# A new task order for a planned one-core kernel (long convolution, then a gated FFN)

## The chip, the core and the metric

The kernel runs on one core of a Trainium2 chip. The metric is the device time of one execution in microseconds (us): the median of three runs, 259.31 us before the change (259.17 to 259.5). The engines carry the profile's names: PE is TensorE (PEld its weight loads), DVE is VectorE, ACT is ScalarE, POOL is GpSimd, SP is SyncE, which here only issues DMAs.

## What is computed

Sequence length S = 2048, width D = 640, FFN width F = 1728, all inputs in bf16. Block A is a gated long convolution, block B a gated FFN behind a LayerNorm.

```python
def _A_ref(q, k, v, shift_k, ssm_k, ssm_D):
    k_pad = jnp.pad(k, ((0, 0), (ks - 1, 0), (0, 0)))          # ks = 4 taps
    for t in range(ks):
        k_shift = k_shift + k_pad[:, t:t + S, :] * shift_k[:, ks - 1 - t][None, None, :]
    kv = k_shift * v
    ...
    y = irfft(rfft(kv_pad) * rfft(ssm_k_pad))[:S]              # causal convolution of length S
    y = y + kv * ssm_D[None, None, :]
    return q * y

def _B_ref(x, w_gate, w_up, w_down):
    return (silu(x @ w_gate) * (x @ w_up)) @ w_down

h = x + _A_ref(_layernorm(x), A_k, A_v, A_shift_k, A_ssm_k, A_ssm_D)      # x is A_q
h2 = h + _B_ref(_layernorm(h), B_w_gate, B_w_up, B_w_down)
```

## The kernel before

The sequence is cut into four blocks of N = 512 tokens. The long convolution is done with block transforms: cosine and sine matrices (`tab` forward, `itab` inverse, `ntab` for the negated half) are multiplied on TensorE with 512 tokens at a time, and the products of transformed blocks j and filters i - j are added up on VectorE. The FFN of block i follows its part of the convolution.

All work is written as some 811 named tasks. `g.add(name, engines, fn, ...)` records one task with what it reads and writes; from that the program derives its dependencies. Nothing in the code decides when a task runs: the strings of `PLAN` do. For each engine (`pe`, `act`, `dve`, `pool`, `sp`) the plan lists task numbers in the order in which the engine runs them, and a task that names two engines ("act dve") runs on the one whose list has it. Every engine works its list strictly in order, and in front of a task it waits for the semaphores of the tasks that it depends on. A DMA belongs to the list of the engine that issues it, most of them to SP.

PSUM is cut into four units of two banks. `PLAN["units"]` gives each TensorE result tile its unit; a tile that opens a unit waits until the other engines have emptied the tile that had the unit before. `PLAN["fills"]` names tasks in front of which TensorE runs constant matmuls (128 x 512, of a tile of ones that the task `zmem` fills, line 492; the matmuls are line 497); their results are never read.

The names that matter here, with the line of the profile:

- `wb0`, `wb4` (L505): five small matmuls that spread the four tap weights of each channel; `diag0`, `diag4` (L511) turn them into diagonal matrices on VectorE. The digits 0, 2, 4 in this and the next names are chunks of 128 channels: 0 stands for chunks 0 to 3 in `wb0` and `diag0`, elsewhere 0 and 2 stand for two chunks each and 4 for one.
- `k0tC.J` (L523): the first block of k, transposed by TensorE (20 transposes); `k0e0`, `k0e2`, `k0e4` (L450, kT<-ps) copy it from PSUM to SBUF. Its data come with the DMAs `k00` and `k02`.
- `tpI.C` (L701): the short convolution of block I, matmuls with the diagonals, 28 for two chunks and 14 for one; `kv0.C` (L719) multiplies block 0 with v on VectorE. For the later blocks `keI.C` (L450, XT<-ps) and `kvI.C` (L712) do it.
- `ktM.P` (L542): the filter block M (loaded as `kcM`), transposed by TensorE, ten transposes each; `kteM.P` (L450, KT<-ps) copies it. `drowadd` (L550) adds ssm_D. `kfM` (L576) transforms the filter, `kfMe` empties PSUM (KO, C, K3r), `kbM` combines (L556).
- `xfI` (L594 for block 0, L614 later): transform of block I, `xfIe` its evacuations (XH, OS), `xbI` (L629) their combination. `pJI` (L747): products. `ybI` (L556, L646): combination ahead of the inverse.
- `ivI.J` (L894 for blocks 0 and 1, L889 later): the inverse, one tile for 128 tokens. `ivI.Je` (L904) on ScalarE evacuates; then come the residual and the LayerNorm (L911, L810, L812, L805, POOL's L807, L951), and `htI.J` transposes the result into `hnT` by a DMA that SP issues.
- `laI` (L797 to L831): first LayerNorm of a block. `xI`, `vI`, `kTI`: loads of q, v and (transposed by the DMA) k for block I.
- `fgI.HG`, `fuI.HG` (L999): gate and up matmuls of block I, half H (256 tokens), group G; 20 matmuls each, 15 for group 3, which is `fg` alone. `sg`, `su`, `sv` (L1007 to L1018) evacuate on ScalarE, `mu` (L1020) multiplies on VectorE, `gd` (L1061) copies 64 rows.
- `dnI.J` (L1085, L962): down projection, `rs` (L1101, L1102, L1106) its evacuation, `ra` (L563, POOL) adds it by DMA to the residual, `out` stores it.
- Weights: `GA`, `UA`, `GB`, `UB`, `PKg`, `PKu` (gate and up), `WdA` to `WdD` (down). They share SBUF with earlier data, so some loads wait.

The first lines of the four compute engines' lists, in names:

```
pe   wb0 k0t0.0 k0t2.0 k0t4.0 k0t0.1 k0t4.1 k0t4.2 k0t2.1 k0t2.2 k0t2.3 wb4 k0t4.3 k0t0.2 k0t0.3 tp0.4 tp0.2 tp0.0 kt0.0 kt0.1 xf0.01 ...
act  wrow warm drow k0e2 k0e4 k0e0 kte0.0 kte0.1 xf0e.01 ...
dve  zmem diag0 diag4 kv0.4 kv0.2 kv0.3 kv0.1 kv0.0 drowadd ...
pool one half halo ...
```

Of the kernel before, what the change touches and what calls it, by code (L numbers as in the profile page):

```python
# [50 lines left out]
class _Graph:  # L51
# [128 lines left out]
    def emit(self, block):  # L180
# [85 lines left out]
    "act":  # L266
# [10 lines left out]
    "dve":  # L277
# [10 lines left out]
    "pool":  # L288
        "16 15 17 125 165 174 158 192 183 223 225 224 342 396 281 371 362 285 401 389 380 289 406 343 293 420 415 466 527 470 "
        "561 474 552 478 579 570 684 529 586 591 705 710 698 637 732 723 641 750 645 741 649 "  # L290
        "",
    "sp":
        "0 2 3 8 4 6 10 7 9 11 231 13 14 296 12 295 230 297 228 234 226 227 235 167 176 229 481 482 233 194 185 232 373 364 286 "
        "282 294 290 391 382 480 653 652 467 563 554 475 471 479 581 572 651 734 725 752 743 638 807 650 801 646 798 642 804 "
# [901 lines left out]
```

## Time and profile before

| | |
|---|---|
| median of three runs | 259.31 us (259.17 to 259.5) |
| the profiled execution, its own time | 258.58 us |
| its span, first to last instruction | 256.4 us |
| busy: PE / DVE / ACT / POOL | 249.6 / 198.3 / 186.5 / 54.2 us |
| constant matmuls (L497) | 7, 3.5 us busy |
| DMA traffic | 35.29 MB, mean 138 GB/s |

How to read the profile's lines below. A line of the timeline has the start in us from the span's start, the duration, the engine, the line of the program, the operation, output <- inputs, a count; in brackets the idle time before it and what ended that. A count above one is a run of like instructions, and a run that a window cuts shows only what lies inside. A line of the groups ends with busy us and the mean ns of one. A line of the windows has the stretch, its length, then the busy time of each engine. Matmuls overlap: the duration of a run includes the last one's way through the array, so that the next run starts before the one ahead of it ends. A line of the chain has start, duration, engine, tile, line and count.

### The profile page before, as it was taken

The numbers are of one execution on the slowest core, as the hardware profiler recorded it, in microseconds if no ns is written. First come the engines' busy times: TensorE is split into PE (matmuls) and PEld (weight loads), VectorE is DVE, ScalarE is ACT, GpSimd is POOL, SyncE is SP. The second block draws the span as 40 slices with busy tenths as digits, with TensorE's granted clock in tenths as the row PEclk, the third lists the DMA queues.
The fourth block names the chain that finished last, engine by engine and source line by source line (L and its number), as shares of the span: only waits on it lengthen the run. The fifth ranks groups of instructions, "written<-read, shape, count | busy, mean of one in ns | idle before, by whom it ended". The sixth has DMA issues, their size and how long they took to land.

```text
span 256.4 us, 5301 instructions
## 1 busy us (share of the span) xinstructions
PE 249.6 (97%) x2256; PEld 195.1 (76%) x2256; DVE 198.3 (77%) x255; ACT 186.5 (73%) x304; POOL 54.2 (21%) x55
## 2 busy tenths in 40 slices
PE   7999997999999999999999999999999999999995
PEld 3778774577888766888888866788886678888763
DVE  2579999999999999999999995999959523012432
ACT  2599999999998698379789799857981847345410
POOL 0002102022313033860031513441130313100000
DMA  6999493889895028877986215499760142400004
GB/s 231 342 313 276 140 379 107 232 168 285 247 196 100 0 45 136 179 130 126 229 174 119 54 27 98 109 214 166 143 119 3 28 77 48 82 1 3 0 19 160
DMA packets 37620, 35.29 MB, mean 138 GB/s; under 512 B 21203, under 2 KB 32478, under 8 KB 37598
## 3 DMA queue, kind: packets, MB, share of 16 engines
q1 hardware_dynamic: 31792, 23.82, 33.1%
q0 software_dynamic: 5792, 11.14, 25.5%
q8 instruction: 17, 0.28, 0.4%
q14 instruction: 5, 0.04, 0.0%
q10 hardware_dynamic: 14, 0.01, 0.0%
HBM read 16.55 MB, written 2.62 MB: 75 GB/s over the span
## 4 chain that ended last, share of the span: by engine, by line
PE 67%; DVE 20%; ACT 8%; DMA 3%; issue 1%
PE ps L999 32%; PE ps L1085 16%; DVE tt L747 6%; PE ps L594 3%; PE ps L576 3%; DVE Y L747 3%; DMA Y<-tt 3%; PE ps L701 3%; PE ps L889 2%; DVE C L747 2%; DVE gu L1020 2%; PE ps L962 2%; PE ps L497 1%; PE ps L614 1%; ACT qo L810 1%; DVE XH L629 1%
## 5 line engine op out<-in xcount | busy, mean ns | idle before, releaser
L1085 PE MATMUL ps<-Wd,gu 128*128 128x320 bf16 (+1 forms) x420 | 58.7, 300 | 0.0
L1085 PEld LDWEIGHTS ps<-Wd,gu 128*128 128x128 bf16 (+1 forms) x420 | 38.8, 97 | 18.4 <-issue 3.6
L747 DVE TENSOR_TENSOR tt<-XH,C 128x2560 bf16<-128x2560 bf16 (+1 forms) x31 | 48.1, 1571 | 0.6 <-ACT XH L450 0.5
L1020 DVE TENSOR_TENSOR gu<-gu,ub 128x1024 bf16<-128x1024 bf16 (+1 forms) x32 | 19.9, 620 | 24.8 <-ACT ub L1012 21.3
L1012 ACT ACTIVATE ub<-ps 128x1024 bf16<-128x1024 f32 x24 | 24.6, 1026 | 18.3 <-PE ps L999 14.0
L1007 ACT ACTIVATE gu<-ps 128x1024 bf16<-128x1024 f32 (+1 forms) x32 | 29.0, 914 | 8.7 <-PE ps L999 8.4
L999 PE MATMUL ps<-hnT,GB 128*128 128x256 bf16 x280 | 33.8, 273 | 0.1
L999 PE MATMUL ps<-hnT,UB 128*128 128x256 bf16 x280 | 33.7, 273 | 0.0
L999 PEld LDWEIGHTS ps<-hnT,GB 128*128 128x128 bf16 x280 | 27.2, 98 | 3.6 <-ACT XT L450 0.2
L999 PEld LDWEIGHTS ps<-hnT,UB 128*128 128x128 bf16 x280 | 27.3, 98 | 3.3
L999 PE MATMUL ps<-hnT,GA 128*128 128x256 bf16 x240 | 28.7, 273 | 0.0
L999 PE MATMUL ps<-hnT,UA 128*128 128x256 bf16 x240 | 28.2, 273 | 0.1
L999 PEld LDWEIGHTS ps<-hnT,UA 128*128 128x128 bf16 x240 | 23.4, 98 | 3.4 <-ACT XH L450 0.5
L999 PEld LDWEIGHTS ps<-hnT,GA 128*128 128x128 bf16 x240 | 23.4, 98 | 3.1 <-ACT C L450 0.2
L810 ACT ACTIVATE qo<-xh 128x640 bf16<-128x640 bf16 x28 | 20.6, 736 | 3.9 <-DVE xh L911 1.6
L807 POOL TENSOR_TENSOR mv<-mv,half 128x1 f32<-128x1 f32 x16 | 14.7, 921 | 35.2 <-DVE mv L805 35.2
L904 ACT ACTIVATE qo<-ps,one,st 128x640 bf16<-128x640 f32 x16 | 13.8, 884 | 9.2 <-PE ps L889 8.9
L576 PE MATMUL ps<-KT,tab 128*128 128x320 bf16 x128 | 19.2, 300 | 0.7 <-ACT K3r L450 0.4
L563 POOL DMA_DIRECT2D xh<-RB x12 | 11.1, 924 | 35.9 <-ACT RB L1101 22.2
L576 PEld LDWEIGHTS ps<-KT,tab 128*128 128x128 bf16 x128 | 11.8, 98 | 6.9 <-ACT KO L450 1.1
L807 POOL TENSOR_TENSOR st<-st,half 128x4 f32<-128x4 f32 x4 | 9.2, 2300 | 31.7 <-DVE st L802 23.2
L450 ACT ACTIVATE XH<-ps 128x640 bf16<-128x640 f32 x18 | 12.6, 712 | 1.4 <-PE ps L614 0.8
(110 smaller groups left out, 385.9 us busy)
## 6 DMA issues: line engine op xcount, KB each, us to landing
C<-US POOLq DMA_DIRECT2D x6, 640.0 KB, 6.3
kc<-in_A_ssm_k_dram SPq DMA_DIRECT2D x4, 640.0 KB, 10.1
xh<-in_A_q_dram SPq DMA_DIRECT2D x4, 640.0 KB, 5.1
out_dram<-xh SPq DMA_DIRECT2D x15, 160.0 KB, 1.9
kvo<-in_A_v_dram SPq DMA_DIRECT2D x3, 640.0 KB, 5.7
xh<-RB POOLq DMA_DIRECT2D x12, 160.0 KB, 3.0
Wd<-in_B_w_down_dram SPq DMA_DIRECT2D x1, 1280.0 KB, 7.4
C<-K3r POOLq DMA_DIRECT2D x2, 640.0 KB, 7.7
```

Of the source, the lines that this page charges most:

```text
L450: return e.activation(out=dst[1], in_=src(), func=ACTF.Copy, scale=scale)
L563: return g.add(name, "pool", lambda e, n: e.dma_start(dst, src, accum_op=ALU.add, max_dma_last_dim=4096), ("acc", 2 * int(np.prod(dst.shap ...
L576: last = e.matmul(pt.f(c, W), tab[:, f, cs, j], src[:, j, c * W:(c + 1) * W], start=(j == js[0]), stop=(j == js[1]))
L747: g.add(nm, "dve", lambda e, n_: e.tensor_tensor(out=d, in0=a, in1=b, op=op), ("sb", n * D), r=[a, b], w=[d])
L807: g.add(name + "r", "pool", lambda e, n: e.tensor_tensor(out=dst, in0=tmp, in1=hf, op=ALU.pow), ("pp", 4), r=[tmp, half[:]], w=[dst])
L810: g.add(name + "m", "act", lambda e, n: e.activation(out=junk, in_=x, func=ACTF.Identity, scale=-1.0 / D, accum_out=sm), ("aa", D, 0), r=[ ...
L904: g.add(nm + "e", "act", lambda e, n, pt=pt, q2=q2, s=s, j=j: e.activation(out=q2, in_=pt.f2(W), func=ACTF.Identity, scale=s[:, 3, j:j + 1 ...
L999: last = e.matmul(pt.f(q // 2, 256, o=256 * (q % 2)), w[:, c, f0:f0 + P], hnT[:, c, cols], start=(c == 0), stop=(c == NC5 - 1))
L1007: g.add("sg%d.%d%d" % (i, h, gp), "act", lambda e, n, pa=pa, gv=gv, nf=nf: e.activation(out=gv, in_=pa.f(0, 256 * nf).rearrange("p (f x) - ...
L1012: g.add("su%d.%d%d" % (i, h, gp), "act", lambda e, n, pb=pb: e.activation(out=ub[:].rearrange("p b x -> p (b x)"), in_=pb.f(0, 1024), func ...
L1020: g.add("mu%d.%d%d" % (i, h, gp), "dve", lambda e, n, gv=gv, ubv=ubv: e.tensor_tensor(out=gv, in0=gv, in1=ubv, op=ALU.mult), ("sb", 256 * ...
L1085: last = e.matmul(pt.f(c, W), gu[k, fb, col(i, j)], Wd[k, fb, c * W:(c + 1) * W], start=st, stop=sp)
```

## The change

The tasks, the shapes, the SBUF addresses and the arithmetic stay; the strings of `PLAN` are new. (The diff also has a second way to do the taps on VectorE, switched off by `DT = ()`, with four buffer names laid over addresses in use; none of its tasks is recorded.)

```diff
     "pe":
-        "20 24 25 26 27 29 32 28 31 34 22 35 30 33 68 65 62 41 39 72 70 48 46 58 54 52 50 56 44 88 80 86 78 137 139 74 82 84 76 "
...
+        "20 22 26 29 24 25 28 32 35 31 34 27 30 33 68 65 62 41 39 72 70 46 56 48 52 50 58 54 44 86 88 78 80 139 84 137 76 74 82 "
...
     "act":
-        "1 18 5 37 38 36 42 40 73 71 49 47 59 55 53 51 45 89 81 87 79 140 75 138 83 85 77 103 97 101 95 105 99 299 91 93 205 "
...
+        "1 18 5 37 36 40 73 71 57 49 53 51 59 55 45 89 79 87 81 140 138 77 85 75 83 97 103 91 93 105 95 101 205 99 302 299 160 "
...
     "dve":
-        "19 21 23 69 66 67 64 63 43 108 109 110 116 117 111 112 113 114 115 118 120 57 119 60 121 61 122 124 128 123 127 129 "
...
+        "23 21 38 69 66 67 64 63 42 43 116 108 109 47 110 112 113 111 117 114 115 118 120 119 121 60 122 61 124 123 126 127 128 "
...
     "pool":
-        "16 15 17 125 165 174 158 192 183 223 225 224 342 396 281 371 362 285 401 389 380 289 406 343 293 420 415 466 527 470 "
...
+        "19 17 15 16 125 165 174 158 192 183 223 225 224 342 396 362 281 371 285 401 380 289 406 389 343 293 420 415 527 466 "
...
     "units":
-        "0012301301013223203222303021212330111020031202211323213232133002231002231231030033310103100121232203201221330332100110"
-        "11232101233001230231203231020221002130200202313022102130221"
+        "0131203132312001201201213230032110213023012230313133033220021021122013200230230222110332013110130232003210332301202110"
+        "01310112312301210312031012210230131023033303012010313012013"
...
     "fills": {
         "wb0": ["zmem", 3],
-        "k0t0.0": ["zmem", 2],
-        "tp0.4": ["zmem", 2],
+        "k0t4.0": ["zmem", 1],
     },
```

In names, what the prediction speaks of. The start of the lists becomes

```
pe   wb0 wb4 k0t4.0 k0t4.1 k0t0.0 k0t2.0 k0t2.1 k0t4.2 k0t4.3 k0t2.2 k0t2.3 k0t0.1 k0t0.2 k0t0.3 tp0.4 tp0.2 tp0.0 kt0.0 kt0.1 xf0.01 ...
act  wrow warm drow k0e2 k0e0 kte0.1 xf0e.01 ...
dve  diag4 diag0 k0e4 kv0.4 kv0.2 kv0.3 kv0.1 kv0.0 kte0.0 drowadd ...
pool zmem halo half one ...
```

`wb4` gets a PSUM unit other than `wb0`'s. Tasks that change engine: `zmem` from DVE to POOL; `k0e4` and `kte0.0` from ACT to DVE; `kf0e.011` to DVE and `kf0e.100` to ACT; later `rs1.2`, `rs1.3`, `rs2.2`, `gd2.0` to DVE and `la3.1x`, `xf3e.30`, `gd3.0`, `gd3.1` to ACT.

From the second inverse tile on, ScalarE's list, up to the task whose end lets the first FFN tile open (marked):

```
before  iv0.1e iv0.0m ke1.4 iv0.0s iv0.1m kf3e.001 iv0.1s iv0.3e kf2e.011 iv0.2e kf2e.111 xf1e.11 kf2e.000 xf1e.00 kf2e.010 xf1e.31 kf2e.001* iv0.3m ...
after   iv0.1e iv0.0m ke1.4 iv0.0s iv0.1m iv0.2e iv0.1s kf3e.001 iv0.3e kf2e.101 kf2e.111 xf1e.30 kf2e.100 kf2e.010 kf2e.001 xf1e.31 kf2e.110 kf2e.011 kf2e.000* xf1e.10 ...
```

and TensorE's, between the last inverse tile of block 0 and the third FFN tile:

```
before  iv0.3 kf2.111 xf1.11 kf2.000 xf1.00 kf2.010 kf2.001 xf1.31 kf2.110 kf2.101 kf2.100 fg0.00 xf1.30 xf1.01 kt3.1 xf1.10 fu0.00 xf1.21 xf1.20 fu0.01
after   iv0.3 kf3.001 kf2.100 kf2.111 xf1.30 xf1.31 kf2.010 kf2.001 kf2.011 kf2.110 xf1.11 kf2.000 xf1.10 xf1.01 fu0.00 xf1.20 xf1.00 fg0.00 xf1.21 fg0.01
```

SP's list, first part, and TensorE's around the transform of block 3:

```
before  ident k00 k02 v0 kc0 tab0 x0 tab1 ntab kc1 PKu kc2 kc3 kT1 itab x1 PKg v1 GB WdC GA UA WdD ht0.0 ht0.1 UB kT2 v2 WdB ht0.3 ht0.2 WdA ht1.1 ht1.0 out0.1 out0.0 ...
after   ident k00 k02 v0 kc0 tab0 x0 tab1 PKg ntab kc1 kc2 kc3 WdD kT1 GA itab UB v1 UA kT2 PKu ht0.0 ht0.1 GB WdC x1 WdB ht0.3 ht0.2 v2 WdA ht1.0 out0.0 ht1.1 out0.2 ...
before  dn1.2 iv2.2 iv2.3 xf3.11 dn1.3 xf3.30 xf3.31 xf3.10 xf3.21 xf3.20 xf3.00 xf3.01 fu2.00
after   dn1.2 iv2.3 iv2.2 dn1.3 xf3.11 xf3.10 xf3.31 xf3.30 xf3.00 xf3.01 xf3.21 xf3.20 fg2.00
```

The last three tasks of TensorE are dn3.3a, dn3.2, dn3.3c in both.

More of the change, by code (lines that the diff above doesn't have):

```diff
@@ L257 @@
     "pe":
[7 rows of a table removed]
[7 rows of a table added]
         "",
     "act":
[9 rows of a table removed]
[9 rows of a table added]
         "",
     "dve":
[9 rows of a table removed]
[9 rows of a table added]
         "",
     "pool":
[L289 to L290 removed]
+        "19 17 15 16 125 165 174 158 192 183 223 225 224 342 396 362 281 371 285 401 380 289 406 389 343 293 420 415 527 466 "
+        "470 561 474 552 478 579 570 684 586 591 529 705 710 698 637 732 723 641 645 750 649 741 "
         "",
     "sp":
[L293 to L294 removed]
+        "0 2 3 8 4 6 10 7 230 9 11 13 14 235 296 226 12 229 297 227 481 231 167 176 228 234 295 233 194 185 482 232 364 282 373 "
+        "290 391 294 286 382 480 653 652 471 563 554 467 475 479 581 572 651 734 725 638 752 646 743 642 650 798 807 801 804 "
         "810 "
@@ L355, in bass_sequential_preLN__ssm_conv_h3__swiglu_ffn__prompt_kernel @@
     BNH = ()
+    DT = ()
+    DTA = ()
     HALF = (0, 1, 2, 3)
@@ L434, in bass_sequential_preLN__ssm_conv_h3__swiglu_ffn__prompt_kernel @@
         one = sb("one", o + 640, [8], f32)
+        kh = sb("kh", SL[2], [7, D])
+        wst = sb("wst", 71680, [D, 4])
+        wbr = sb("wbr", 174336, [4, D])
+        tm = sb("tm", 71680, [4, 2, D])
         wrow = sb("wrow", 99840, [NC5, 64, 4])
@@ L682, in kvload @@
         def kvload(i):
+            if i in DT:
+                load("wst", wst[:].rearrange("p d u -> p (d u)"), bass.AP(A_shift_k.tensor, A_shift_k.offset, [[0, P], [1, 4 * D]]), 655360)
+                load("kh%d" % i, kh[:].rearrange("p j d -> p (j d)"), bass.AP(K2.tensor, K2.offset + (N * i - 3) * D, [[4 * D, P], [1, 7 * D]]), 1146880)
+                load("v%d" % i, kvo[:], tokens(V2, i), 655360)
+                return
             tload("kT%d" % i, kT[:], K2[N * i - 16:N * (i + 1), :], N + 16, D)
@@ L686, in taps @@
         def taps(i):
+            if i in DT:
+                g.add("wbr", "act", lambda e, n: e.activation(out=wbr[:], in_=wst[:].rearrange("p d u -> p u d"), func=ACTF.Copy), ("ac", 4 * D), r=[wst[:]], w=[wbr[:]])
+                for j0 in (1, 0):
+                    kin = kh[:, 3 + j0]
+                    kin = bass.AP(kin.tensor, kin.offset, [list(kin.ap[0]), [-D, 4], [2 * D, 2], [1, D]])
+                    win = wbr[:].unsqueeze(2).to_broadcast([P, 4, 2, D])
+                    vj = kvo[:, j0:4:2, :]
+                    nm = "tv%d.%d" % (i, j0)
+                    g.add(nm + "a", "dve", lambda e, n, kin=kin, win=win: e.tensor_tensor(out=tm[:], in0=kin, in1=win, op=ALU.mult), ("sb", 8 * D),
+                          r=[kh[:], wbr[:]], w=[tm[:]])
+                    if i in DTA:
+                        addto(nm + "b", tm[:, 0:2], tm[:, 2:4])
+                    else:
+                        g.add(nm + "b", "dve", lambda e, n: e.tensor_tensor(out=tm[:, 0:2], in0=tm[:, 0:2], in1=tm[:, 2:4], op=ALU.add), ("sb", 4 * D),
+                              r=[tm[:]], w=[tm[:, 0:2]])
+                    g.add(nm + "c", "dve", lambda e, n: e.tensor_tensor(out=tm[:, 0], in0=tm[:, 0], in1=tm[:, 1], op=ALU.add), ("sb", 2 * D),
+                          r=[tm[:, 0:2]], w=[tm[:, 0]])
+                    g.add(nm + "d", "dve", lambda e, n, vj=vj: e.tensor_tensor(out=vj, in0=tm[:, 0], in1=vj, op=ALU.mult), ("sb", 2 * D),
+                          r=[tm[:, 0], vj], w=[vj])
+                return
             ks = kT if i else kT0
```

44 rows, old and new, of the table PLAN are left out of this document.

## The prediction

> **What bounds the kernel now.** I read the page's busy shares, then stretches cut where the limiting engine changes, then the timeline of each stretch.
>
> ```profile
> span 256.4 us, 5301 instructions
> PE 249.6 (97%) x2256; PEld 195.1 (76%) x2256; DVE 198.3 (77%) x255; ACT 186.5 (73%) x304; POOL 54.2 (21%) x55
> ...
> 0.00:12.90 12.90, 11.03 (x122) 6.94 (x123) 5.30 (x8) 4.87 (x6) 0.42 (x7) 1.00 0.86 287
> 12.90:37.70 24.80, 24.80 (x252) 18.81 (x254) 22.74 (x32) 23.91 (x33) 2.21 (x1) 1.00 0.94 274
> 37.70:53.00 15.30, 13.56 (x109) 8.28 (x108) 15.30 (x18) 15.27 (x29) 1.60 (x2) 1.00 0.68 188
> 53.00:113.80 60.80, 60.43 (x558) 48.91 (x558) 60.60 (x68) 51.11 (x87) 22.35 (x18) 1.00 0.70 147
> 113.80:149.00 35.20, 35.20 (x352) 29.46 (x352) 35.16 (x39) 29.92 (x49) 7.91 (x5) 1.00 0.66 133
> ```
>
> The columns are the stretch and its length, the busy time of PE, PEld, DVE, ACT and POOL, and the granted clock. TensorE has work for the whole span, so time is won or lost only where it starts late or idles. It idles in the first 12.9 us (1.87 in all) and between 37.7 and 53 (1.74, while ScalarE is busy for 15.27 of 15.30); from there to 149 it is out of work for 0.4 us. Up to 149 VectorE is nearly as full: it idles 2.06 between 12.9 and 37.7 and hardly at all after that, so a gain on TensorE alone would run into VectorE.
>
> **The start.**
>
> ```profile
> 2.84 1.06 PE L505 MATMUL ps<-wrow,idall 2*128 2x256 bf16 x4
> 3.84 1.04 PE L497 MATMUL ps<-gu 128*128 128x512 bf16 x2
> 4.31 0.10 PEld L523 LDWEIGHTS ps<-idall,k0n 128*128 128x128 bf16 x1 [0.35 <-DMA k0n<-in_A_k_dram]
> 4.66 1.81 PE L523 MATMUL ps<-idall,k0n 128*128 128x128 bf16 x15
> 6.40 0.39 PE L505 MATMUL ps<-wrow,idall 2*128 2x256 bf16 x1
> 6.73 0.71 PE L523 MATMUL ps<-idall,k0n 128*128 128x128 bf16 x5
> 7.31 1.04 PE L497 MATMUL ps<-gu 128*128 128x512 bf16 x2
> 8.28 2.96 PE L701 MATMUL ps<-diag,kT 64*128 64x256 bf16 x70
> 11.17 1.31 PE L542 MATMUL ps<-idall,kc 128*128 128x128 bf16 x20
> 12.90 0.85 PE L594 MATMUL ps<-kvo,tab 128*128 128x320 bf16 x5 [0.43 <-DVE kvo L719]
> ...
> 108.74 2.47 PE L701 MATMUL ps<-diag,kT 64*128 64x256 bf16 x70
> ```
>
> ```profile
> 3.94 1.22 DVE L511 TENSOR_TENSOR diag<-idall,ps 128x1024 bf16<-128x1024 bf16 x1 [2.55 <-PE ps L505]
> 6.83 0.42 DVE L511 TENSOR_TENSOR diag<-idall,ps 128x256 bf16<-128x256 bf16 x1 [1.67 <-PE ps L505]
> ...
> 10.36 2.48 DVE L719 TENSOR_TENSOR kvo<-ps,v 128x512 bf16<-128x512 f32 x4 [0.30 <-PE ps L701]
> 13.23 0.48 DVE L550 TENSOR_TENSOR KT<-KT,drow 1x640 bf16<-1x640 bf16 x1 [0.38 <-ACT KT L450]
> ...
> 6.51 2.43 ACT L450 ACTIVATE kT<-ps 128x1024 bf16<-128x1024 bf16 x3 [3.69 <-PE ps L523]
> 11.96 2.37 ACT L450 ACTIVATE KT<-ps 128x1280 bf16<-128x1280 bf16 x2 [3.02 <-PE ps L542]
> ```
>
> The first transform (12.90) waits for the last of five products (kv0). Four run in one stretch of 2.48 from 10.36, when the second tap group (tp0.2) has ended. That group stands behind the first (tp0.4, 8.28), which stands behind two constant matmuls (7.31) and needs ScalarE's copies of the transposed k (from 6.51). Beside this, wb4 (6.40) and its diagonal (6.83) come late, because wb4 shares a PSUM unit with wb0 and waits until the first diagonal is out (3.94 + 1.22).
>
> In the new order wb4 has a unit of its own and follows wb0 at once. A wb matmul takes (1.06 - 0.39)/3 = 0.22, so wb4 starts at 2.84 + 4 x 0.22 = 3.73 and ends by 4.15. Then comes one constant matmul: 0.1 for the change of kind (3.84 less 3.73), 0.43 for itself (two took 1.04 with the last one's drain), and k0t4.0 starts at 4.48, after its data (4.31). The transposes take (1.81 - 0.71)/10 = 0.11 each; unbroken by wb4, the twenty are issued by 6.6, and no constant matmuls follow. On VectorE the small diagonal (from 4.17) and the large one end by 5.75, and k0e4 follows; k0e2 on ScalarE starts at 6.2 instead of 6.51. So tp0.4 starts at 6.72 instead of 8.28: 1.56 earlier.
>
> Not all of that is kept. The 70 matmuls of the taps took 2.96 here and 2.47 at 108.74: 0.49 lost, so the first us of them ran at half rate, up to about 9.3. If the switch comes at the same time, the first 42 of the 70, now starting earlier, run at half rate throughout: 42/70 x 2 x 2.2 (2.47 without the drain) = 2.6. So tp0.2 is issued by 9.3 and drained by 9.6, against 10.36. Four products at 2.48/4 = 0.62 then end at 12.1. The third group ends by 10.5, before its products' turn at 10.8, and the 20 kc0 transposes (1.31) fit in before 12.1. **Term: the first transform at 12.1 instead of 12.9, -0.8.** Of the three constant matmuls saved none counts by itself: they lay in the waits for the copies.
>
> Not shown: a copy out of PSUM by VectorE in these shapes. The diagonals give (1.22 - 0.42)/768 = 1.04 ns per column, so 0.69 for k0e4 (512 columns) and 1.5 for kte0.0 (1280), which I take because they are copies out of PSUM too. The bounds come from VectorE's rows for 640 columns, out of SBUF (0.38) and out of PSUM (0.88), scaled: 0.3 to 0.7 for k0e4, 0.76 to 1.76 for kte0.0.
>
> ```profile
> L821 DVE TENSOR_SCALAR xh<-xh,mvs 128x640 bf16<-128x640 bf16 x4 | 1.5, 379 | 0.0
> L1102 DVE TENSOR_SCALAR RB<-ps,st 128x640 bf16<-128x640 f32 x3 | 2.6, 881 | 0.0
> L489 POOL MEMSET kT<- 128x80 bf16 x1 | 0.2, 165 | 0.0
> ...
> 0.72 0.10 POOL L488 MEMSET one<- 128x8 f32 x1 [0.29 <-POOLq L1181]
> ```
>
> No value of k0e4 delays tp0.4, which TensorE reaches at 6.72. The zmem fill on POOL, which the three opening constant matmuls need, is not shown either: 0.06 for 72 more elements gives 0.5 for 512, between 0.17 (the row for 80) and 1.06 (the same, times 512/80). I take 0.5, by the difference of two rows: the fill ends at 1.25, the three matmuls by 2.6, and wb0 starts at 2.84 as before. At 1.06 all starts 0.25 later.
>
> The granted clock reads 1.00 throughout, yet transposes took 0.11 each at 4.66 and 20 of them 1.31 in all at 11.17, so the half rate is real. [...]
>
> **From 12.1 to the first inverse.** TensorE is full, so the term carries if VectorE keeps up. VectorE takes kte0.0 (1.5), which the same engine waited 0.38 for before, and swaps one kf0 evacuation with ScalarE (no difference).
>
> ```profile
> 33.59 1.50 DVE L556 TENSOR_TENSOR OS<-Y 128x2560 bf16<-128x2560 bf16 x1
> ...
> 35.77 1.93 PE L894 MATMUL ps<-OS,itab 128*128 128x320 bf16 x13
> ```
>
> The inverse (it started at 35.36, three of its matmuls at (1.93 - 0.85)/8 = 0.135 before the quoted row, which is cut by its window) needs yb0.0, which ended 35.09. By the new order: the products end at 12.1 (12.84 before, 10.36 + 2.48), kte0.0 at 13.6, and drowadd starts there, 0.4 later than before (13.23). Of the 2.06 that VectorE idled in this stretch 0.38 was the wait for kte0.0; the other 1.7 lay before evacuations that TensorE now delivers 0.8 earlier, so most of the 1.5 is taken up there. I put yb0.0's end at 34.3 (35.09 - 0.8) and TensorE's need at 34.6 (35.36 - 0.8): hidden by 0.3. If the idle takes up less, the rest stands in front of the inverse; that is rival C.
>
> **ScalarE's stretch.**
>
> ```profile
> 49.11 2.08 PEld L999 LDWEIGHTS ps<-hnT,GA 128*128 128x128 bf16 x20 [0.21 <-ACT C L450]
> ...
> 50.37 1.19 ACT C L450 x2
> ...
> 5.59 0.90 SPq L442 DMA_DIRECT2D PK<-in_B_w_up_dram  x1
> 43.32 2.54 SPq L445 DMA_TRANSPOSE hnT<-qo  x2
> 46.53 5.62 SPq L445 DMA_TRANSPOSE kT<-in_A_k_dram  x1
> hnT<-qo SPq DMA_TRANSPOSE x16, 2.7
> ```
>
> ScalarE has no idle here, so TensorE gets a PSUM unit back whenever one of its tasks ends, and the order of those tasks decides when the FFN, which needs few evacuations for its long matmuls, can begin. Before, the first FFN tile (49.11) opens behind the 17th task counted from the second inverse tile's evacuation; in the new order it is the 19th (iv0.1e to kf2e.000). Two evacuations at 1.19/2 = 0.6 are +1.2. TensorE uses that time for two more xf1 tiles (4 x 0.135 = 0.55) that would have come later, and the waits behind the opening, 0.2 and less each, shrink by about 0.1. **Term: +0.5** (0 if the mix of tasks meets TensorE better, +1.2 if the two tiles only wait).
>
> On SP, kT2 (5.62) and PKu (0.90) now stand ahead of ht0.0 and ht0.1, and SP does nothing else while kT2 waits for its buffer, which tp1.4 reads in the first us of this stretch. From about 37.8 that is 44.3 for both, 46.9 for the two hnT transposes (2.54); the second lands 2.7 after it starts, at 48.3, before the tile at 49.5: hidden by 1.2. GA and UB go ahead of v1, which waits for the same buffer as before, so they cost it nothing; x1, WdC and GB go behind ht0.1, several us ahead of their users. Later ht1.1 stands behind out0.0, which waits for an accumulation; I give its tile less than 1 us of cover and no price.
>
> **The rest.**
>
> ```profile
> 113.78 0.39 PEld L614 LDWEIGHTS ps<-kvo,tab 128*128 128x128 bf16 x4 [0.41 <-DVE kvo L712]
> ...
> 149.08 1.26 PE L889 MATMUL ps<-Y,itab 128*128 128x320 bf16 x8
> ...
> 159.30 2.53 PE L614 MATMUL ps<-kvo,tab 128*128 128x320 bf16 x14
> 161.66 1.58 PE L999 MATMUL ps<-hnT,UA 128*128 128x256 bf16 x13
> ```
>
> At 113.8 TensorE waited about 0.3 for VectorE, at 149.08 0.1. VectorE's chain up to there has the same work in both orders and comes 0.8 earlier, TensorE only 0.3 (0.8 - 0.5), so TensorE no longer waits: **-0.4**. At 159.30, 14 matmuls take 2.36 to the next tile where 14 x 0.137 would be 1.9. In the new order all eight xf3 tiles follow dn1.3 and one waits for rs1.3 on VectorE (0.88): **+0.2**. The other tasks that change engine (rs1.2, rs2.2, gd2.0, gd3, la3.1x) do so after 149, where no stretch is bound by ScalarE or VectorE, and the last three matmul tasks stay as they were.
>
> Sum: -0.8 + 0.5 - 0.4 + 0.2 = -0.5. Span 256.4 becomes 255.9. That execution took 258.58 (2.18 outside the span), so 258.1; the runs' median is 0.73 higher, 259.31, so **258.8**.
>
> **Rivals.**
>
> B. ScalarE gives nothing back, because the reordered evacuations meet TensorE better; VectorE sets the time and the front's gain stays, or full rate comes earlier (if it holds for half of the 42 tap matmuls, 0.65 more). -0.8 to -1.4: 258.2. For: VectorE full to 149. Against: 19 tasks, no idle.
>
> C. Slower: VectorE is late for the first inverse. It took over 2.2 us of copies and has 0.3 to spare there. If its idle time takes up none of kte0.0, yb0.0 ends 1.5 later than I put it and iv0.0 starts 1.2 later, and with it ScalarE's whole stretch and VectorE's full stretch to 149. The sum is then -0.8 + 1.2 + 0.5 - 0.4 + 0.2 = +0.7: 260.0. It decides from 0.5 late at the inverse, where the sum is zero. For it speaks the small margin, against it 2.06 of idle.
>
> D. The front does not do what it says, because the half rate lasts longer with three constant matmuls fewer. If it lasts beyond the kc0 transposes, the third tap group takes 28/70 x 2 x 2.2 = 1.8 (to 11.1) and the transposes 20 x 0.11 = 2.2, so the transform starts at 13.3 instead of 12.1: 260.0 with the other terms; at half the delay 259.4. For it: the transposes that fill the gap ran at half rate for 2.8 us without ending it. Against: the taps, which follow earlier now, are no transposes.
>
> **How the numbers follow.** Forecast 45% (own range 258.4 to 259.3), B 22%, C 21%, D 12%. This measurement can tell about 0.2%, 0.5 us, from no change. The forecast lies on that bound: 22% faster, 22% same, 1% slower; B all faster; C 3% same, 18% slower; D 4% same, 8% slower, by 0.5. Together 44, 29 and 27. The range, 257.6 to 260.4, holds B down to -1.4 with a little to spare below, C's and D's prices, and the POOL fill at its bound.
>
> **What would show it.** Right: tp0.4 near 6.7, first transform near 12.1, no [idle <-DVE OS] at the first inverse, first FFN tile near 49.5, no wait near 113. Wrong: the transform after 12.7, a VectorE wait before the first inverse, or an FFN tile waiting for hnT's DMA.

## The result, and the profile after

In 22 runs each the changed kernel took 258.26 us (median; 256.98 to 259.45) and the kernel before 259.07 (258.05 to 260.14): ratio 0.9969, 95% interval 0.9954 to 0.9984, or -0.8 us. In a second set (12 and 35 runs) it was 258.54 against 258.87, ratio 0.9991 (0.9963 to 1.002). The forecast was 258.8 by a gain of 0.5, in a range of 257.6 to 260.4. (Executions over 1.5% above a kernel's fastest are left out of all ratios here; where they matter below, their spans are told.)

One profiled execution can mislead at this size. The first one of the changed kernel has a span of 257.3, where the kernel before has 256.4: by the two traces alone the change would cost 0.9. It was one of the slowest of the 22 runs. A second one, of the same program (e1_again), has 256.1. So the readings below go by what several executions share.

The timeline of TensorE at the start, changed kernel:

```profile
2.76 1.29 PE L510 MATMUL ps<-wrow,idall 2*128 2x256 bf16 x5
3.99 0.61 PE L502 MATMUL ps<-gu 128*128 128x512 bf16 x1
4.66 2.31 PE L528 MATMUL ps<-idall,k0n 128*128 128x128 bf16 x20
6.90 3.80 PE L731 MATMUL ps<-diag,kT 64*128 64x256 bf16 x70
...
12.24 1.94 PE L599 MATMUL ps<-kvo,tab 128*128 128x320 bf16 x13 [0.30 <-DVE kvo L749]
```

and VectorE's:

```profile
4.09 1.55 DVE L516 TENSOR_TENSOR diag<-idall,ps 128x256 bf16<-128x256 bf16 x2 [4.09 <-PE ps L510]
5.94 0.69 DVE L457 COPY kT<-ps 128x512 bf16<-128x512 bf16 x1 [0.30 <-PE ps L528]
...
9.70 2.48 DVE L749 TENSOR_TENSOR kvo<-ps,v 128x512 bf16<-128x512 f32 x4 [0.79 <-PE ps L731]
12.10 0.81 DVE L457 COPY KT<-ps 128x1280 bf16<-128x1280 bf16 x1
```

Both wb matmuls now run at once, nothing breaks the 20 transposes, the taps start at 6.90 (8.28 before) and the first transform at 12.24 (12.90). The taps took 3.80, though 2.96 before: half rate lasted longer here. (The change from half to full rate is called the switch below.) In the second execution it ended sooner (TensorE, then VectorE's products):

```profile
6.69 2.74 PE L731 MATMUL ps<-diag,kT 64*128 64x256 bf16 x70
10.50 1.31 PE L547 MATMUL ps<-idall,kc 128*128 128x128 bf16 x20 [1.06 <-DMA kc<-in_A_ssm_k_dram]
12.05 2.21 PE L599 MATMUL ps<-kvo,tab 128*128 128x320 bf16 x15 [0.24 <-DVE kvo L749]
...
8.90 3.08 DVE L749 TENSOR_TENSOR kvo<-ps,v 128x512 bf16<-128x512 f32 x5 [2.48 <-DMA v<-in_A_v_dram]
```

All 70 taps at full rate take 2.47, so the rest, twice, is the time at half rate: it ended at 6.90 + 2 x (3.80 - 2.47) = 9.6 in the first execution and at 6.69 + 2 x 0.27 = 7.2 in the second, with the same program. What the early switch gained, late loads took back: that of the first filter (the 1.06 at 10.50) and above all that of v, for which the five products waited until 8.90. The transform waits for the last of them.

At the first inverse and the first FFN tile, changed kernel, first execution:

```profile
32.93 1.49 DVE L561 TENSOR_TENSOR OS<-Y 128x2560 bf16<-128x2560 bf16 x1
...
34.48 1.80 PE L924 MATMUL ps<-OS,itab 128*128 128x320 bf16 x12
...
49.46 2.08 PEld L1029 LDWEIGHTS ps<-hnT,UA 128*128 128x128 bf16 x20 [0.48 <-ACT C L455]
```

No wait for OS stands at the inverse, and the FFN opens at 49.46. Two stretches of the same execution (length, then PE, PEld, DVE, ACT, POOL busy):

```profile
36.82:52.20 15.38, 13.31 (x102) 7.81 (x101) 15.00 (x17) 15.38 (x30) 2.38 (x2) 1.00 0.66 166
52.20:114.47 62.27, 60.91 (x567) 48.96 (x564) 60.77 (x68) 51.02 (x87) 26.43 (x19) 1.00 0.72 149
```

and the second of them in e1_again:

```profile
52.00:113.28 61.28, 60.86 (x566) 48.96 (x564) 60.68 (x68) 50.97 (x87) 26.46 (x19) 1.00 0.72 151
```

ScalarE is busy throughout its stretch, as before. In the long one TensorE idles 1.36 and 0.42, VectorE 1.50 and 0.60, for the same work. Around 110 the two executions part. First VectorE, TensorE and ScalarE in the first one:

```profile
100.05 1.49 DVE L777 TENSOR_TENSOR tt<-XH,C 128x2560 bf16<-128x2560 bf16 x1 [0.90 <-DMA Y<-tt]
...
107.69 2.83 DVE L777 TENSOR_TENSOR C<-XH,C 128x5120 bf16<-128x5120 bf16 x1
110.55 2.43 ACT L455 ACTIVATE XT<-ps 128x1024 bf16<-128x1024 f32 x3 [1.14 <-DVE C L777]
111.63 2.36 PE L1029 MATMUL ps<-hnT,GB 128*128 128x256 bf16 x20 [0.88 <-ACT XT L455]
114.47 0.72 PE L619 MATMUL ps<-kvo,tab 128*128 128x320 bf16 x4 [0.48 <-DVE kvo L742]
```

then the second:

```profile
98.88 1.49 DVE L777 TENSOR_TENSOR tt<-XH,C 128x2560 bf16<-128x2560 bf16 x1
...
110.50 2.36 PE L1029 MATMUL ps<-hnT,GB 128*128 128x256 bf16 x20
113.28 0.72 PE L619 MATMUL ps<-kvo,tab 128*128 128x320 bf16 x4 [0.42 <-DVE kvo L742]
```

The accumulation Y<-tt (p02.e) landed at 100.03 in the first and at 98.19 in the second; 15 of its 16 parts were there by 97.80 and 97.62, so one late part makes the difference. VectorE waited 0.90 for it in the first execution and ran without a gap from there, so its last product that reads XH ended that much later (107.69 + 2.83 = 110.52). XT lies at XH's address, so ScalarE could write XT only then (110.55), and TensorE got its PSUM unit late: 0.88 for a DMA two engines away.

Later in the first execution, at the transform of block 3 (TensorE, then VectorE):

```profile
159.71 0.98 PE L619 MATMUL ps<-kvo,tab 128*128 128x320 bf16 x6
160.93 1.69 PE L619 MATMUL ps<-kvo,tab 128*128 128x320 bf16 x10 [0.24 <-DVE mv L835]
...
159.99 0.89 DVE L1132 TENSOR_SCALAR RB<-ps,st 128x640 bf16<-128x640 f32 x1 [0.49 <-PE ps L1115]
```

One of the eight tiles waits for a unit that rs1.3 (L1132) empties on VectorE, as the new order has it. (The profile names mv, which ran right behind; rs1.3 ended at 160.88, the tile began at 160.93.)

Five places, by execution: when the first transform starts, then the time from it to the first FFN tile of block 1 (fu1.00), to the first tile of block 2's transform (xf2.30), and to the last store.

| execution | transform | to fu1.00 | to xf2.30 | to last store |
|---|---|---|---|---|
| before | 12.90 | 91.37 | 9.52 | 140.53 |
| before again (e5) | 13.12 | 91.36 | 10.00 | 140.52 |
| changed, first | 12.24 | 91.57 | 10.66 | 140.76 |
| changed, second (e1) | 12.05 | 91.58 | 9.65 | 140.76 |
| changed, no constant matmuls (e11) | 12.00 | 91.58 | 9.65 | 140.75 |
| front alone (e2) | 12.09 | 91.48 | 10.24 | 140.52 |
| front alone (e12) | 11.36 | 91.35 | 9.90 | 140.52 |

The times to fu1.00 and from xf2.30 to the last store repeat within 0.13 for each order: +0.21 and +0.24 for the new one. The transform, and the time from fu1.00 to xf2.30, vary between executions of one program.

### The profile page after: what moved, and what is told of

Its sections match the earlier page's. It is cut to its first block, busy times and chain, and to the rows that moved or that the text cites. A ratio compares the mean times of both kernels' runs of the same rounds, so it can differ in the third digit from the quotient of the medians.

```text
span 257.3 us, 5303 instructions
## 1 busy us (share of the span) xinstructions
PE 249.3 (97%) x2253; PEld 195.1 (76%) x2253; DVE 200.0 (78%) x256; ACT 184.5 (72%) x302; POOL 58.5 (23%) x56
## 4 chain that ended last, share of the span: by engine, by line
PE 62%; DVE 20%; ACT 11%; DMA 5%; issue 1%; SPq 0%; DVEq 0%
PE ps L1029 32%; PE ps L1115 16%; DVE tt L777 6%; PE ps L599 3%; DMA Y<-tt 3%; DVE Y L777 3%; PE ps L731 2%; ACT KO L455 2%; PE ps L919 2%; ACT C L455 2%; PE ps L581 2%; DVE C L777 2%; PE ps L992 2%; PE ps L619 2%; DMA k0n<-in_A_k_dram 1%; DVE gu L1050 1%
## 5 line engine op out<-in xcount | busy, mean ns | idle before, releaser
L1037 ACT ACTIVATE gu<-ps 128x1024 bf16<-128x1024 f32 (+1 forms) x32 | 29.4, 923 | 12.1 <-PE ps L1029 12.0
L837 POOL TENSOR_TENSOR mv<-mv,half 128x1 f32<-128x1 f32 x16 | 21.3, 1335 | 24.7 <-DVE mv L835 24.7
L837 POOL TENSOR_TENSOR st<-st,half 128x4 f32<-128x4 f32 x4 | 7.9, 1986 | 33.6 <-DVE st L832 21.8
L455 ACT ACTIVATE XH<-ps 128x640 bf16<-128x640 f32 x19 | 13.3, 736 | 1.5 <-PE ps L619 0.7
```

Source lines behind the costliest of these rows:

```text
L455: return e.activation(out=dst[1], in_=src(), func=ACTF.Copy, scale=scale)
L837: g.add(name + "r", "pool", lambda e, n: e.tensor_tensor(out=dst, in0=tmp, in1=hf, op=ALU.pow), ("pp", 4), r=[tmp, half[:]], w=[dst])
L1037: g.add("sg%d.%d%d" % (i, h, gp), "act", lambda e, n, pa=pa, gv=gv, nf=nf: e.activation(out=gv, in_=pa.f(0, 256 * nf).rearrange("p (f x) - ...
```

## The experiments

**e1_again**: the changed kernel, no edit.

> The changed kernel once more, for a second profiled execution. In the first one TensorE waits 1.0 at 110.6 and 0.65 at 113.7 although the prediction had these waits gone; ahead of them VectorE idles 0.90 at 100.05 for the accumulation Y<-tt (p02.e), which took 8.4 from issue to landing where the kernel before has 6.8. Theory 1: this landing varies from execution to execution, and the medians (-0.8 us) come from executions with less of it: the second profile shows a landing near 7, VectorE idle under 0.3 there, a wait of TensorE under 0.5 in 110 to 114, and a span near 256. Theory 2: the new order of POOL and SP makes the landing late in every execution: again 8 or more and 0.9 idle, and the span near 257.3. Time against the kernel before: 0.997 (0.995 to 0.9985) by both.

Span 256.1, no wait for Y<-tt: theory 1, the landing varies. The ratio, 0.9991, is above what both theories gave. The wait ahead of 113.28 stayed (0.42 idle). Three of the 12 spans were 258.2 to 259.8, which no theory had; e4 has a likely cause.

**e2_front and e12_front2**: the new order for the first 51 tasks only. kte0.0 starts inside them and so is on VectorE.

```diff
-pe   wb0 k0t0.0 k0t2.0 ... tp0.4 tp0.2 tp0.0 kt0.0 kt0.1 | ...
+pe   wb0 wb4 k0t4.0 ... tp0.4 tp0.2 tp0.0 kt0.0 kt0.1 | as before
-act  wrow warm drow k0e2 k0e4 k0e0 kte0.0 kte0.1 | ...
+act  wrow warm drow k0e2 k0e0 kte0.1 | as before
-dve  zmem diag0 diag4 kv0.4 ... kv0.0 | ...
+dve  diag4 diag0 k0e4 kv0.4 ... kv0.0 kte0.0 | as before
```

> The new order for the first 51 tasks alone (up to the start of the first transform: wb4, the order of the k0t transposes, k0e4 on VectorE, zmem on POOL, the constant matmuls, PKg earlier on SP), the old order from there; kte0.0 stays on ScalarE only if its start lies behind that point. Forecast's theory: the front is worth -0.8 and the rest of the change costs +0.3, so this part alone gives -0.8: ratio 0.997, the transform at 12.2 (12.9 before), the first inverse at 34.5 (35.36), the first FFN tile at 48.3 (49.11). Rival V: VectorE, full from 33 to 149, sets the time, and the old order of its tasks gives the gain back at 111 to 149: ratio 0.999 to 1.000, with waits of TensorE for VectorE of 0.5 or more there.

258.00 us, ratio 0.9953 (0.9933 to 0.9973). The transform came at 12.09, the inverse at 34.55, the FFN at 48.31: the front's gain goes through ScalarE's stretch whole. But in this execution rival V was at work too. The rows at 97 (VectorE) and 111 (TensorE):

```profile
97.67 0.45 DVE L980 TENSOR_SCALAR qo<-xh,mv 128x640 bf16<-128x640 bf16 x1 [0.40 <-POOL mv L836]
...
111.32 2.36 PE L1028 MATMUL ps<-hnT,GB 128*128 128x256 bf16 x20 [0.81 <-ACT XT L454]
```

VectorE waits for a power on GpSimd, and 14 us later TensorE pays: 10.24 from fu1.00 to xf2.30. The same program again:

> The front alone, the same program as e2_front, for a second interval and a second profiled execution. Theory: its gain over the kernel before is the largest so far and holds: ratio 0.994 to 0.997, no span over 257.5, so it is faster than the changed kernel (0.997 and 0.999 in two sets of runs) because it lacks the executions with the long power of la1r and what ScalarE's stretch gives back. Rival V (VectorE takes the gain back at 110, as in its first profiled execution, where the gain of 0.81 was 0.02 from 114 on): ratio 0.998 to 1.000.

257.67 us, ratio 0.9945 (0.9925 to 0.9966), no span over 255.9. Of 1.54 gained at the transform against the first execution of before, 0.38 went at 110 (TensorE waits 0.48 for XT there), and 1.19 reached the last store. So rival V takes a part, and not the whole by the medians. The front alone has the lowest ratios of the study, but their intervals overlap that of e11 and that of the changed kernel's first set.

**e3_rest and e7_rest4**: the old front, the new order behind it; e7 with four constant matmuls instead of seven.

```diff
         "wb0": ["zmem", 3],
-        "k0t0.0": ["zmem", 2],
-        "tp0.4": ["zmem", 2],
+        "k0t0.0": ["zmem", 1],
```

> The old order up to the first transform (with its constant matmuls, and zmem on VectorE), the new order behind it. Forecast's theory: +0.5 in ScalarE's stretch, +0.2 at xf3, -0.4 for vanished waits: +0.3, ratio 1.001, the first FFN tile near 50.3. Rival B (ScalarE gives nothing back): ratio 1.000 or below. Rival W (the accumulation Y<-tt is late by the new order): VectorE idles 0.9 before p12.0a, TensorE waits over 1 us in 110 to 114, ratio 1.004 to 1.006.

260.49 us, ratio 1.0054 (1.0025 to 1.0083): far over the +0.3, and not by rival W, since VectorE did not wait ahead of p12.0a. The places show 91.60, 9.64 and 141.11: the last is 0.35 above the changed kernel's. That is the wait at xf3 again, 0.60 here (at 160.27) and in e7 where the changed kernel has 0.24: rs1.3 began 0.48 after the last matmul of dn1.3 (158.85 to 159.32), in the changed kernel 0.12. Why is not shown. The DMA view of this kernel from 254 to 258 has a code load (q8) and one store:

```profile
q8 instruction: 1, 0.02, 2.2%
issues: line engine op xcount, KB each, median us to landing
out_dram<-xh SPq DMA_DIRECT2D x1, 80.0 KB, 2.9
```

The same store takes 1.6 in e1_again, where no code load falls there; here one of its parts landed at 257.47, the others by 256.1, and the span is longer for it.

> The rest of the change alone, as before (old front, new order behind it), but with four constant matmuls in the front (three ahead of wb0, one ahead of k0t0.0) in place of seven, so that TensorE's program is shorter by three pairs. In the rest alone a code load (q8, 16 KB) fell at 255.0 on the final store (issued at 254.56), and one of its 16 parts landed at 257.47 in place of 256.1; its span was 1.3 longer for it. Theory (the code load sets the extra 1.1 to 1.4 us of the rest alone, and constant matmuls do nothing): no code load in the last 2 us, the final store lands in 1.6, the span near 256.6, ratio 0.999 to 1.001. Rival (the order itself costs 1.3): ratio 1.004 to 1.006 with the store landing in 1.6. Rival D (three constant matmuls fewer let the half rate last longer): first transform at 13 or later, ratio 1.006 or more.

260.04 us, ratio 1.0032 (1.0011 to 1.0053). No code load met the store, which landed in 1.6, but the time hardly fell, so that theory does not account for the rest's price. What did show is rival D at the transform, though the ratio stays below the 1.006 that D asked for. TensorE in e7 (only the start of this execution is read; it later had e4's wait too):

```profile
7.64 4.44 PE L730 MATMUL ps<-diag,kT 64*128 64x256 bf16 x70 [0.64 <-ACT kT L454]
...
13.48 0.72 PE L598 MATMUL ps<-kvo,tab 128*128 128x320 bf16 x4 [0.15 <-DVE kvo L748]
```

TensorE idled 0.64 ahead of tp0.4, and half rate lasted through the taps, to 7.64 + 2 x 1.97 = 11.6, and the transform came at 13.48. Its spans fall in three groups, 256.2 to 256.3 (2), 257.5 to 258.1 (8) and 261.6 to 261.8 (2, the profiled one among them). That late switches make the middle group is likely, not shown. Why the rest alone costs 0.8 to 1.4 by the ratios, where its three places (e3) add 0.5 to 0.9 to those of before, stays open.

**e4_const and e8_const2**: two constant matmuls put back into the changed kernel.

```diff
         "k0t4.0": ["zmem", 1],
+        "tp0.4": ["zmem", 2],
```

> The changed kernel with two constant matmuls (128 x 512) put back in front of tp0.4, six in all instead of four (seven before). Forecast's theory: full rate comes at the same time whatever fills TensorE before, so the two only take their own 0.43 each at half rate, part of it in the wait for the copies: tp0.4 0.4 to 0.8 later, the transform up to 0.5 later, ratio to the kernel before 0.997 to 0.999. Rival D (constant matmuls bring full rate earlier): the 70 tap matmuls take 2.7 or less in place of the changed kernel's, and the transform stays at 12.2 or comes earlier, ratio 0.995 to 0.997.

259.71 us, ratio 1.0042 (1.0012 to 1.0072): slower than both theories said. The taps took 2.50, the transform came at 12.34. Its profiled execution has a span of 260.3 (GpSimd, VectorE, ScalarE and TensorE of e4):

```profile
77.87 10.68 POOL L838 TENSOR_TENSOR st<-st,half 128x4 f32<-128x4 f32 x1 [1.88 <-DVE st L836]
...
84.83 2.83 DVE L778 TENSOR_TENSOR Y<-XH,C 128x5120 bf16<-128x5120 bf16 x1
...
88.64 1.66 ACT L935 ACTIVATE qo<-ps,one,st 128x640 bf16<-128x640 f32 x2 [3.77 <-POOL st L838]
89.58 1.73 PE L925 MATMUL ps<-Y,itab 128*128 128x320 bf16 x8 [2.74 <-ACT qo L935]
91.11 4.13 PE L1116 MATMUL ps<-Wd,gu 128*128 128x320 bf16 x20
```

la1r raises 4 numbers per partition to a power. It took 1.40 in both executions of the changed kernel and in those of e3, e8 and e11, which have the same order here, and 10.68 in this one (and in e7); the inverse of block 1 waits for it. It ended 0.89 after VectorE had run out of work (87.66). Spans about 2 or more above the median stand in 3 of 12 runs here and as many in e1; that the same power makes those is likely, not shown. In the first 22 runs of the changed kernel there are none, none in e11, and none with the old order at this place (e2, e5, e9, e10, e12).

> The changed kernel with two more constant matmuls ahead of tp0.4, the same program as e4_const, for a second profiled execution: the first one was an execution with the long power of la1r (2.9 us of waiting), so that what makes the other executions 1.2 us slower than the changed kernel was not to be seen. Theory 1: a fixed place where a code load meets a transfer that is waited for (p02.e or the final store), which the two matmuls moved: a wait of 0.7 to 1.3 at that place, while the first transform is at 12.3 (12.05 to 12.24 in the changed kernel). Theory 2: the front itself, by a transform at 12.9 or later. Ratio 1.003 to 1.006 by both.

259.04 us, ratio 1.0015 (0.9993 to 1.0037). The transform came at 11.73 and no such place as theory 1 asked for exists: from fu1.00 on the trace is that of the changed kernel (9.66, 140.75). Both theories miss; that the price lies in executions with a late switch, where the two run at half rate, is open, since both profiled ones switched early.

**e5_before**: the kernel before, no edit.

> The kernel before, unchanged, against itself: ratio 1.000, interval within 0.9975 to 1.0025. In five profiled executions so far the first full-rate matmul came at 9.35 (before), 9.81 and 7.35 (the changed kernel twice), 9.22 (front alone), 8.15 (rest alone, which has the old front), whatever constant matmuls ran ahead. Theory (the switch falls at a random time): in this second execution of the kernel before it falls anywhere between 7 and 10, and the first transform follows it: 12.2 with a switch before 8.3, 12.9 with one after 9.3. Rival D (the seven constant matmuls set it): 9.35 +- 0.2 and the transform at 12.9 again.

Ratio 0.9993 (0.9972 to 1.0014): the comparison is good to about 0.2%. Its TensorE:

```profile
8.28 3.17 PE L701 MATMUL ps<-diag,kT 64*128 64x256 bf16 x70
...
13.12 1.12 PE L594 MATMUL ps<-kvo,tab 128*128 128x320 bf16 x7 [0.43 <-DVE kvo L719]
```

The switch at 8.28 + 2 x 0.70 = 9.7, the transform at 13.12: it follows the switch, as the theory says, further than the two values it gave.

**e6_order**: two tasks of VectorE moved in the changed kernel.

```diff
-dve  ... p11.1c la1v mu0.02 p11.1e mu0.03 yb1.0 mu0.10 yb1.1 p02.d p02.a iv1.0g p02.c mu0.11 p02.b mu0.12 ...
+dve  ... p11.1c mu0.02 p11.1e mu0.03 la1v yb1.0 mu0.10 yb1.1 p02.d p02.a iv1.0g p02.c p02.b mu0.11 mu0.12 ...
```

> The changed kernel with two tasks of VectorE moved: la1v from behind p11.1c to just ahead of yb1.0 (its old neighbourhood), and p02.b ahead of mu0.11 and mu0.12, so that the accumulation p02.e is issued 0.7 earlier. Theory: two things that hit the changed kernel only in some executions go away, the GpSimd power behind la1v (la1r: 1.40 in three executions, 10.68 in the fourth, where TensorE then waited 2.9), and VectorE's wait for p02.e. No span over 257.5 (3 of 12 of the changed kernel were at 258.2 to 259.8), the median 0.2 to 0.6 below the changed kernel's, ratio 0.9955 to 0.997. Rival: the long power has another cause, or it only moves: spans of 258 and more as before, ratio 0.998 to 1.000.

261.50 us, ratio 1.0101 (1.0071 to 1.0131): the theory fell. The smallest span is 258.4, so what was rare became the rule. GpSimd and VectorE:

```profile
79.93 8.34 POOL L836 TENSOR_TENSOR st<-st,half 128x4 f32<-128x4 f32 x1 [3.76 <-DVE st L834]
...
84.56 2.82 DVE L776 TENSOR_TENSOR Y<-XH,C 128x5120 bf16<-128x5120 bf16 x1
```

Again the power ends 0.89 after VectorE's last operation (87.38; in e4 87.66), as if it had been held up until VectorE stopped. That is an estimate from these two rows, and it can't be the whole cause: in the changed kernel the power took 1.40 while VectorE ran the same operations, also without a gap. Why it took 8.34 here, and 2.25 with the old neighbours (80.36, kernel before), is not shown.

**e9_to35 and e10_to54**: the new order up to the first inverse, and up to 54, the old one behind it.

```diff
-every list: first 51 tasks new (front alone)
+every list: tasks started before 34.4 (e9) or 54 (e10) new
```

> The new order up to the first inverse (34.4), the old order from there: the front, kte0.0 on VectorE, and the new order of the transforms of block 0 and its filter. In the two profiled executions of the changed kernel the first inverse came another 0.21 earlier than the first transform (-0.88 and -1.07 for -0.67 and -0.86); with the front alone both were -0.81. Theory: front and this 0.2 carry to the end: first transform 12.05 to 12.25 unless the switch comes after 10, first inverse 34.3 to 34.5, first FFN tile 48.1 (49.11 before), no long power of la1r, ratio 0.9945 to 0.9965. Rival C (VectorE, with kte0.0 added, is late at or behind the first inverse): first inverse 0.3 or more behind yb0.0's old distance, waits of TensorE for VectorE at 110 over 1.0, ratio 0.998 or more.

258.40 us, ratio 0.9975 (0.9959 to 0.9992): between the two expectations and no better than the front alone. This execution had an early switch and an early filter load:

```profile
6.60 2.69 PE L730 MATMUL ps<-diag,kT 64*128 64x256 bf16 x70
...
10.96 2.35 PE L598 MATMUL ps<-kvo,tab 128*128 128x320 bf16 x16 [0.18 <-DVE kvo L748]
...
34.02 2.35 PE L923 MATMUL ps<-OS,itab 128*128 128x320 bf16 x16 [0.76 <-ACT XT L454]
```

Of the 1.94 gained at the transform, 1.35 were left at the first FFN tile (47.77): in the first inverse TensorE waited 0.76 for ScalarE, with the new order of the tasks ahead of it. In e12, with the old one, the inverse came at 33.81 without such a wait.

> The new order up to 54, the old one from there: the kernel of e9 plus the new order of ScalarE's stretch. Forecast's theory: the stretch gives back 0.4 to 0.5, so the first FFN tile comes near 49.4 and what follows 0.4 to 0.5 later than in e9, ratio 0.0015 to 0.002 above e9's (0.996 to 0.9985). Rival B (it gives nothing back): the tile within 0.1 of its place by e9's gain when the matmuls done ahead of it are counted, ratio equal to e9's.

259.50 us, ratio 1.0020 (0.9999 to 1.0042). Its time says nothing of the stretch: where the orders join, TensorE waits 0.67 (at 55.16) and 0.68 (at 56.29) for ScalarE, which neither kernel does. Ahead of that its first FFN tile came 14.99 after the inverse, as in the changed kernel; in the old order it is 13.76.

**e11_none**: no constant matmul.

```diff
     "fills": {
-        "wb0": ["zmem", 3],
-        "k0t4.0": ["zmem", 1],
     },
```

> The changed kernel without any constant matmul (four in the changed kernel, seven before). The first full-rate matmul came at 7.35, 7.7, 9.22 and 9.81 in executions of the new front with four, at 7.4 and 8.3 with six, at 8.15, 9.35 and 9.75 in the old front with seven, and at 12.0 in the old front with four, where TensorE stood idle for 0.95 ahead of tp0.4. Rival D (too little work of TensorE ahead of the taps puts the switch off): the switch at 10 or later, the first transform at 13 or later, in most executions, ratio 0.6% to 1% above the changed kernel's (1.002 to 1.006). Forecast's theory (the constant matmuls don't count): the switch between 7.3 and 9.9 and the transform at 12.0 to 12.3, ratio 0.996 to 0.999.

258.14 us, ratio 0.9959 (0.9939 to 0.9979), at least as fast as with four. TensorE:

```profile
6.65 3.96 PE L728 MATMUL ps<-diag,kT 64*128 64x256 bf16 x70
...
12.00 2.21 PE L596 MATMUL ps<-kvo,tab 128*128 128x320 bf16 x15
```

The switch came at 6.65 + 2 x 1.49 = 9.6 and the transform at 12.00. D, which puts the switch at 10 or later and the transform at 13, fell here, by one trace and by the median.

## Why the prediction was right

**The front.** The step held: POOL's fill 0.52 (0.5), wb4 and the diagonals done at 5.64 (5.75), k0e4 0.69 (0.69), tp0.4 at 6.90 and 6.69 (6.72), the transform at 12.24 and 12.05 (12.1). kte0.0 was mis-sized: 0.81 in place of 1.5. The row for two-input diagonals gave the small copy exactly and was wrong for the large one, whose lower bound of 0.76 came closer. The weak step was "if the switch comes at the same time" (9.3). It came at 7.2 and 9.6 in two executions of the changed kernel, at 9.3 and 9.7 in two of the kernel before, and at 7.0 to 9.0 in those of e2, e6, e9, e10 and e12. At like times the gain is about the forecast's: 12.09 (e2, switch at 9.0) against 12.90 (before, 9.3), and 11.62 (e10, 8.2) against 12.21 (e3, where all 70 taps, from 8.07, ran at full rate). Over eight executions of the new front (four or no constant matmuls) the mean is 11.80, over three of the old one 12.74: **-0.9** for -0.8.

**To the first inverse.** Rival C fell: the copies took 1.5 of VectorE, not 2.2, and no wait stands there. The 0.3 to spare did not exist, though: yb0.0 ended at 34.42 (forecast 34.3), the inverse began at 34.48. TensorE came 0.2 sooner than reckoned: 22.24 from the transform to the inverse in place of 22.45, for the same 234 matmuls without a gap. Before, filter transforms and transposes stood between the two tap groups (31.54 and 34.32); in the new order the 56 taps run in one stretch (from 32.52) and take 1.96 to the start of the next group in place of 1.03 + 1.04, and the last ten transposes take 0.56 (31.32) in place of 0.65 (33.67). That is the 0.2. I gave this no price. With 0.06 to spare it was luck that kte0.0 was short: at 1.5, yb0.0 would have ended up to 0.7 later (an estimate; VectorE idles 1.14 between the transform and the inverse, which could take some of it up).

**ScalarE's stretch.** The FFN opened at 49.46 (49.5), 14.99 after the inverse in place of 13.76: the two evacuations more, +1.2. From the first inverse to fu1.00 the changed kernel needs 69.33 and 69.35 where the kernel before needs 68.91: +0.43 for +0.5. With the 0.2 just named that is the +0.21 of the table. Rival B's first clause fell. Its second, full rate earlier, came true in the second execution (7.2), but there the loads held the transform at 12.05.

**The waits at 113.8 and 149.** This is the step that failed. -0.4 was forecast, because VectorE would come 0.8 earlier and TensorE 0.3, so that TensorE no longer waits. The wait ahead of xf2.30 grew instead. TensorE in the kernel before, then VectorE in the second execution of the changed one:

```profile
111.30 2.36 PE L999 MATMUL ps<-hnT,GB 128*128 128x256 bf16 x20
113.79 0.72 PE L614 MATMUL ps<-kvo,tab 128*128 128x320 bf16 x4
...
42.72 0.45 DVE L981 TENSOR_SCALAR qo<-xh,mv 128x640 bf16<-128x640 bf16 x1 [0.38 <-POOL mv L837]
95.56 0.45 DVE L981 TENSOR_SCALAR qo<-xh,mv 128x640 bf16<-128x640 bf16 x1 [0.46 <-POOL mv L837]
```

Before, TensorE was idle for 0.13 there (113.66 to 113.79), and 0.13 in every old order that was profiled; with the new order it is 0.41 to 0.48 wherever la1r was short. The time from fu1.00 to xf2.30 was 9.65 for 9.52, +0.13, and the wait near 149 stayed as well. VectorE did come earlier and lost it again, in waits for GpSimd's powers of 0.38 at 42.7 and 0.46 at 95.6. The first stands in no execution with the old order at its place and, at 0.37 to 0.38, in every one with the new (e3 too, with the old front), so it belongs to the order and not to the earlier start. A wait like the second comes in some executions of the old order too (0.44 at 99.3 in e5). The two powers took 1.87 and 1.47, in the kernel before 0.92 and 0.75. The first execution also waited for p02.e. I had counted VectorE's work and not what it waits for on GpSimd. How much the step is worth stays open: in the other old-order executions of the table TensorE also waits 0.48 to 0.81 for XT ahead of this place, which then takes 9.90 to 10.24. Against these the new order's 9.65 is the forecast's -0.3 to -0.6, though not for the reason given.

**xf3.** +0.24 for +0.2, the same in the three executions of the whole new order in the table, and by the wait for rs1.3 that was named; +0.59 with the old front (e3).

Sum: -0.9 + 0.2 + 0.1 + 0.2 = -0.4; the medians say -0.8 and -0.3. The forecast came out right in sign and size in part by luck: the term that was 0.5 off was nearly made up by what the sum left out (-0.2 at the transforms), by the front (-0.1) and by the stretch (-0.1). With -0.3 in place of +0.1 at the failed step the sum would be -0.8, so the two sets of runs lie within what the traces leave open. The first set's 258.26 is also rival B's 258.2, and the traces speak against B; and 0.24 of its distance from 258.8 is the starting point, 259.31 in three runs, 259.07 in 22.

## What to carry to other kernels

Where an earlier start is the aim, look at what is next in line behind it, on every engine that hands a buffer back: here ScalarE at 34 (e9) and VectorE's late XH at 110 (e2, e12) took part of what the front had gained. Test the parts alone: the first 51 tasks (0.9945 and 0.9953) were worth at least as much as the whole reordering (0.9969 and 0.9991), though the intervals overlap in part. And where the gain is 0.3%, take a second profile before explaining the first: the changed kernel's two differ by 1.2 us, more than the change is worth.

## What the runs showed of the hardware

The half rate ended at 7.2 and 9.6 in two executions of one program, by the taps' durations; why they differ by 2.4 is not shown. A transpose took (1.81 - 0.71)/10 = 0.11 at the half rate (4.66, kernel before) and (1.28 - 0.72)/10 = 0.056 later in the changed kernel (20 at 18.77, ten at 22.06). The clock record in the trace of the first execution starts only at 9.82 (the first full-rate matmuls of the two came at 9.81 and 7.35), so the granted clock of 1.00 that the views give for the start does not cover the half rate. The prediction set against rival D that the taps are no transposes. In the second execution, behind one constant matmul (0.61 from 4.02) and 20 transposes (2.34 from 4.42), the rate rose about 0.5 us into the taps (6.69 to 7.2); in the first, behind the same, about 2.7 into them (6.90 to 9.6). No run shows that taps and transposes differ in this.

Half rate also comes back in the middle of a kernel, and here the views show it (e4; the stretch, its length, PE, PEld, DVE, ACT and POOL busy, then the granted clock):

```profile
86.80:90.20 3.40, 0.66 (x6) 0.47 (x6) 1.49 (x3) 1.56 (x3) 1.75 (x1) 1.00 0.00 0
90.22:93.63 3.41, 3.41 (x15) 1.90 (x14) 3.23 (x3) 2.80 (x7) 0.00 (x0) 0.50 0.00 0
```

After the wait of 2.74, 20 matmuls of a down projection took 4.13 (91.11) where the changed kernel needs 2.88 (87.63). In the stretch of 3.40 ahead of 90.22 TensorE was busy for 0.66 and idle for 2.74, at a granted clock of 1.00; in the next one the clock was 0.50. More of the cause is not shown.

A power of four numbers on GpSimd took 1.40 or 10.68 us with the same operations of VectorE beside it, and a 16 KB code load that fell together with the last store (e3) went with 1.3 us more for that store.
